# Query products of a linear-attention block on a block diagonal with a doubled k^T v, in a fused attention and two-stage MoE kernel

## The chip, the cores and the metric

The kernel runs on one core of a Trainium2 chip. The metric is the device time of one execution in microseconds. A NeuronCore has five engines that run on their own: TensorE (PE, with its weight loads listed as PEld), VectorE (DVE), ScalarE (ACT), GpSimd (POOL) and SyncE (SP, here the queue that issues most transfers).

## The reference, cut to what matters

Eight batches of eight heads go through linear attention without softmax, then through an RMS norm per head. The result feeds a first mixture of experts (top 1 of 8, routed by a cosine) and a second one (a balanced assignment).

```python
def _attn_ref(q, k, v, g_norm):          # q, k, v: (8, 8, 576, 64) float32
    kv = np.einsum('bhsd,bhse->bhde', k, v)
    out = np.einsum('bhsd,bhde->bhse', q, kv)
    rms = np.sqrt(np.mean(out * out, axis=-1, keepdims=True) + 1e-06)
    return (out / rms * g_norm).astype(np.float32)
...
    x = np.ascontiguousarray(attn_out.transpose(0, 2, 1, 3)).reshape(B * S, H * D)
    x = _moe_ref(x=x, **moe_kwargs)      # logits = normed x @ normed expert_emb.T / tau
    return _moe2_ref(x=x, **moe2_kwargs)
```

## The kernel before

The kernel is one function with nested helpers; all instructions are issued in program order, and each engine works through its own in that order. The attention part is at the start of the span, up to about 141 us; the two mixtures of experts fill the rest.

**k^T v.** Batches are handled in four groups of two (gi = 0 to 3). For each batch, `kv(b)` (L255) multiplies the 576 rows of k and v of each head in nine chunks of 64 rows (L265, matmuls on 64x64 quarters of the array), four heads to a PSUM tile, two such halves per batch (hg). ACT copies a half to the tile `kvn` (L272), and for the first half DVE copies it a second time (L274). Then eight matmuls per batch (L287, 64 rows by 128 columns of weights, 80 columns moving) multiply it by `gex`. `gex` (L210, filled by `gate_weights` at L230 to L237) holds, beside an identity, the routing vectors of the experts for two heads. So one product both moves k^T v into place and multiplies it by the routing weights. DVE and ACT copy its halves to `kvx` (L291, L292), one of four buffers that batches use in turn. `kvh` (L251) picks the columns of one head in one half of the partitions: 64 columns of k^T v and 8 columns of logits, KW = 72 in all.

**Query products.** A step is one unit: one pair of 128-row blocks (u = 0 to 3, four heads hg) or a tail of 64 rows per batch (u = 4). There are ten steps per group, forty in all, listed by `steps`. `qa` (L299) transposes four 128x128 blocks of q on PE (L310); each transposed block has two rows of a token pair r = 0, 1 above one another, so partitions 0 to 63 belong to r = 0 and 64 to 127 to r = 1. ACT copies them to `qT` (L311). `qb` (L314) multiplies for each head h and each r a 64x128 block of weights from `qT` with the 72 columns of `kvh` (L329, eight matmuls per unit; for u = 4 L336 with 64x64 blocks). Every f32 matmul that is not a transpose shows in the trace as two loads and two matmul passes, so a unit has sixteen of each. The PSUM pool `mm` that holds products, k^T v and later the expert layers has two buffers.

**Evacuation.** DVE or ACT (a list `EVAC` decides) copies the values to `x` (L347, L349), ACT squares them (L352) and copies the logits to `lp` (L355), and one step later DVE sums the squares (L359, `late`). In the last group ACT does the copy of every unit.

**Order.** Step n first starts a `kv` of the next group at the steps named in `KVAT`, transposes for step n + 2 (`qa`), issues loads of q, then runs `qb` of step n, then one piece of every generator in `bg` (`pump`): `kv` and `group_end`. `group_end` (L363) makes the norm, the routing and the slot tables of the group before on DVE, POOL and PE (L467, L468, L507). In the last group the steps also cast the first expert weights (ACT L553, DVE L559). After the steps, `first0` (L949) fills PE with the first expert's layers (L678 to L680, L720 to L722) while DVE and POOL finish the tables and the gathers, and the transposes L645 take the gathered rows. `warm` (L849, L852) runs transposes at the start. At the start POOL also fills constants (L188, L581, L699) and token numbers (L860, L863) that DVE splits (`split64`, L866).

The groups of 64-row matmuls differ in array shape: transposes and expert layers use 128x128, L329 and L287 use 64x128, L265 and L336 use 64x64.

Of the kernel before, what the change touches and what calls it, by code (L numbers as in the profile page):

```python
# [7 lines left out]
F32 = mybir.dt.float32  # L8
# [3 lines left out]
AF = mybir.ActivationFunctionType  # L12
OP = mybir.AluOpType
AX = mybir.AxisListType
# [57 lines left out]
def fused_kernel(ctx, tc, q, k, v, g_norm, emb, tau, w1, w2, wgate, v1, v2, out):  # L72
    nc = tc.nc
    V = nc.vector
    B, H, S, D = q.shape
    HD = H * D
    HP = H // 2
    E = emb.shape[0]
# [22 lines left out]
    def mk(pool, shape, dtype, name, **kw):  # L101
        if pool is mp:
            pool = MP[name in MP0]
        return pool.tile(shape, dtype, name=name, **kw)

    def con(shape, dtype, name):
        return consts.tile(shape, dtype, name=name)
# [8 lines left out]
    gp = grp.enter_context(tc.tile_pool(name="grp", bufs=1, side="right"))  # L116
    att = ExitStack()
    ap = att.enter_context(tc.tile_pool(name="att", bufs=2, side="right"))
# [49 lines left out]
    ident = con([128, 128], F32, "ident")  # L168
# [26 lines left out]
    def run_gen(g):  # L195
        for _ in g:
            pass

    def rsqrt(o, u, y, w):

        nc.scalar.activation(w, u, AF.Sqrt)
        yield
        V.reciprocal(y, w)
        V.tensor_tensor(w, u, y, op=OP.mult)
        V.scalar_tensor_tensor(w, w, -0.5, y, op0=OP.mult, op1=OP.mult)
        V.scalar_tensor_tensor(o, w, 1.5, y, op0=OP.add, op1=OP.mult)

    gex = mk(gp, [128, 2, E + D + E], F32, "gex")  # L210

    def gate_weights():
        emsq = mk(ap, [128, 8, D], F32, "sq").rearrange("p a c -> p (a c)")[:E, :HD]
        en2 = con([E, 4], F32, "en2")
        V.tensor_tensor(emsq, em, em, op=OP.mult)
        V.tensor_reduce(en2[:, 0:1], emsq, axis=AX.X, op=OP.add)
        V.tensor_scalar(en2[:, 1:2], en2[:, 0:1], 1e-36, None, op0=OP.max)
        run_gen(rsqrt(en2[:, 2:3], en2[:, 1:2], en2[:, 3:4], emsq[:, 0:1]))
        V.tensor_tensor(en2[:, 0:1], en2[:, 0:1], en2[:, 2:3], op=OP.mult)
        V.tensor_scalar(en2[:, 0:1], en2[:, 0:1], 1e-6, tau8, op0=OP.add, op1=OP.mult)  # L220
        V.reciprocal(en2[:, 0:1], en2[:, 0:1])
        emh = em.rearrange("p (h d) -> p h d", h=H)
        V.scalar_tensor_tensor(emh, emh, en2[:, 0:1], gB[:E, None, :].to_broadcast([E, H, D]),
                               op0=OP.mult, op1=OP.mult)
        yield
        pe_ = mk(psum, [64, H, E], F32, "sm")
        for h in range(H):
            nc.tensor.transpose(pe_[:, h, :], em[:, h * D:(h + 1) * D], ident[:E, :E])

        for c in range(2):  # L230
            V.tensor_copy(gex[64 * c:64 * c + 64, :, E:E + D],
                          ident[64 * c:64 * c + 64, None, 64 * c:64 * c + 64].to_broadcast([64, 2, D]))
            for s in range(2):
                h = 2 * (c ^ s) + s
                g = gex[64 * c:64 * c + 64, s]
                V.tensor_copy(g[:, :E], pe_[:, h])
                V.tensor_copy(g[:, E + D:], pe_[:, h + 4])  # L237


    KW = D + E  # L240
# [4 lines left out]
    V.memset(run, 0.0)  # L245
    NKV = 4


    kvx = [mk(ap, [128, 2, 2, 2, KW + E], F32, f"kvx{i}", bufs=1) for i in range(NKV)]

    def kvh(b, h, r):  # L251
        hg, a, s = h // 4, h // 2 % 2, h % 2
        return kvx[b % NKV][64 * r:64 * r + 64, a ^ s, s, hg ^ r, E * hg:E * hg + KW]

    def kv(b):  # L255

        kvn = mk(ap, [128, 2, 3, D], F32, "kvn", bufs=2)
        for hg in range(2):
            p = mk(psum, [128, 2, 512], F32, "mm")
            kt, vt = LD["k", b, hg], LD["v", b, hg]  # L260
            for r in range(KR):
                for s in range(2):
                    for a in range(2):
                        c = s ^ a
                        nc.tensor.matmul(p[64 * c:64 * c + 64, s, :D],  # L265
                                         vt[64 * s:64 * s + 64, a, r, :], kt[64 * s:64 * s + 64, a, r, :],
                                         start=(r == 0), stop=(r == KR - 1))
            m = 2 * b + hg + NL
            if m < 2 * B:
                load_main(m // 2, "k", m % 2)  # L270
                load_main(m // 2, "v", m % 2)
            nc.scalar.copy(kvn[:, :, hg], p[:, :, :D])  # L272
            if hg == 0:
                V.tensor_copy(kvn[:, :, 2], p[:, :, :D])  # L274
            yield
            if hg == 0:
                yield
        if b > 0:
            yield

        W = KW + E
        p = mk(psum, [128, 2, 512], F32, "mm")
        for s in range(2):
            for o in range(2):
                for c in range(2):
                    i = 2 * s + o
                    nc.tensor.matmul(p[:, c, i * W:(i + 1) * W],  # L287
                                     kvn[64 * c:64 * c + 64, s, o:o + 2].rearrange("p h d -> p (h d)"),
                                     gex[64 * c:64 * c + 64, s], start=True, stop=True)
        x = kvx[b % NKV].rearrange("p c s o w -> p c (s o w)")  # L290
        V.tensor_copy(x[:, 0], p[:, 0, :4 * W])  # L291
        nc.scalar.copy(x[:, 1], p[:, 1, :4 * W])  # L292
        yield

    GS = {}
# [18 lines left out]
    def qb(gi, u, hg, late):  # L314
        if u == 0 and hg == 0:
            GS[gi] = dict(s1=mk(gp, [128, TG * H], F32, "s1", bufs=2), lp=mk(gp, [128, TG * H, E], F32, "lp", bufs=2))
        if hg == 0:
            GS[gi]["x", u] = mk(gp, [128, 2, XP], F32, "xo", bufs=8) if u < 4 else mk(gp, [128, 1, XP], F32, "xt", bufs=2)
        G = GS[gi]
        j, rr = divmod(u, 2)  # L320
        qT = QT.pop((gi, u, hg))
        po = mk(psum, [128, 2, 512], F32, "mm")
        n = 8 if u < 4 else 4
        if u < 4:

            ov = po[:, :, :4 * KW].rearrange("p r (h w) -> p r h w", h=4)
            for h in range(4):
                for r in range(2):
                    nc.tensor.matmul(ov[:, r, h], qT[64 * r:64 * r + 64, h, :], kvh(2 * gi + j, 4 * hg + h, r),  # L329
                                     start=True, stop=True)  # L330
        else:
            ov = po[:, :, :2 * KW].rearrange("p a (c w) -> p a c w", w=KW)
            for h in range(2):
                for s in range(2):
                    for jj in range(2):
                        nc.tensor.matmul(ov[64 * jj:64 * jj + 64, s, h],  # L336
                                         qT[64 * s:64 * s + 64, h, 64 * jj:64 * jj + 64],
                                         kvh(2 * gi + jj, 4 * hg + 2 * h + s, s), start=True, stop=True)

        vs, ls = (slice(E, KW), slice(0, E)) if hg == 0 else (slice(0, D), slice(D, KW))  # L340
        o3 = po[:, :, :n // 2 * KW].rearrange("p a (c w) -> p a c w", w=KW)
        sq = mk(ap, [128, 8, D], F32, "sq")
        x = G["x", u]
        c0 = u * 16 + hg * n
        cp = nc.scalar.copy if (gi, u, hg) in EVAC else V.tensor_copy
        if u < 4:
            cp(x[:, :, hg * 4 * D:(hg + 1) * 4 * D].rearrange("p r (h d) -> p r h d", h=4), ov[:, :, :, vs])  # L347
        else:
            cp(x[:, 0, hg * 4 * D:(hg + 1) * 4 * D].rearrange("p (c s d) -> p s c d", s=2, c=2), ov[:, :, :, vs])  # L349
        if late is not None:  # L350
            late()
        nc.scalar.activation(sq[:, :n].rearrange("p (a c) d -> p a c d", a=2), o3[:, :, :, vs], AF.Square)  # L352

        o = "p (c a) n -> p a c n" if u < 4 else "p (a c) n -> p a c n"
        nc.scalar.copy(G["lp"][:, c0:c0 + n].rearrange(o, a=2), o3[:, :, :, ls])  # L355

        def later():
            o = "p (c a) -> p a c" if u < 4 else "p (a c) -> p a c"
            V.tensor_reduce(G["s1"][:, c0:c0 + n].rearrange(o, a=2), sq[:, :n].rearrange("p (a c) d -> p a c d", a=2),  # L359
                            axis=AX.X, op=OP.add)  # L360
        return later

    def group_end(gi):  # L363
# [534 lines left out]
    for n, st in enumerate(steps):  # L898
        gi, u, hg = st
        i = n % len(UNITS)  # L900
# [502 lines left out]
    a = logits_w(e6, 0)  # L1403
    xtiles(0, e7, 2, 3)
    a()
    b = logits_w(e6, 1)
# [99 lines left out]
    a = logits_w(e7, 1)  # L1506
# [182 lines left out]
```

## Time and profile before

| what | value |
|---|---|
| runs shown | median 1156.23 us, 1155.98 to 1157.61, three runs |
| profiled execution | 1156.87 us, its span 1155.1 us |
| PE busy | 1106.5 us (96%), 8819 matmuls |
| DVE, ACT, POOL busy | 618.5, 448.7, 299.0 us |
| mean granted TensorE clock | 0.95 of full |
| bytes moved | 153.03 MB, mean 132 GB/s |

A busy time is the union of an engine's instructions. Matmuls overlap, so a PE that is busy all the time need not be at its peak; the granted clock (1.0 is 2.4 GHz, 0.5 is 1.2 GHz) is shown beside it. In a line of the timeline the first number is the start in us from the span's start, the second how long the merged run lasts, and square brackets give idle time of the engine before it and what ended it. "issue" means that the engine waited for nothing that the profile shows.

### The profile page before, as it was taken

To read this page: it belongs to the slowest core of one execution; us is meant where nothing else is said; L and a number is where in the kernel's file an instruction comes from. 1 tells how busy PE (TensorE), PEld (TensorE's weight loads), DVE (VectorE), ACT (ScalarE), POOL (GpSimd) and SP (SyncE) were. 2 spreads that over 40 slices of the span, in tenths; PEclk is the share of its full clock that TensorE was granted. 3 is DMA by queue.
4 is the path that set the end of the run, shared out by engine and by line. 5 is a ranking of instruction groups with operands and counts; after the bars stand their busy time and mean duration, and the time that the engine had idled before them with its cause. 6 is when DMAs were issued, how large, how long until landed. Compare 5 with 4: busy or idle time off the path is not lost. (4 is left out here: it accounts for less than half of the span.)

```text
span 1155.1 us, 21545 instructions
## 1 busy us (share of the span) xinstructions
PE 1106.5 (96%) x8819; PEld 1019.8 (88%) x8819; DVE 618.5 (54%) x1319; ACT 448.7 (39%) x801; POOL 299.0 (26%) x374
## 2 busy tenths in 40 slices
PE   8899997999999999999989988999999999999998
PEld 7677787999999999999879878989898998989896
DVE  3366875387778686868546671615243433425140
ACT  2365635543535363545431221424233332425130
POOL 0011436425142332415003332112213030203101
PEclk8787588999999999999999888999999999999999
DMA  9997545442525343434120123515153433424201
GB/s 286 380 341 243 197 143 176 137 144 83 175 88 160 103 145 118 128 115 129 55 77 2 44 75 99 159 60 188 55 174 99 147 119 112 140 90 156 87 29 41
DMA packets 94532, 153.03 MB, mean 132 GB/s; under 512 B 11080, under 2 KB 52040, under 8 KB 94416
## 3 DMA queue, kind: packets, MB, share of 16 engines
q1 hardware_dynamic: 85456, 122.18, 33.1%
q0 software_dynamic: 8960, 29.30, 7.9%
q8 instruction: 73, 1.20, 0.4%
q14 instruction: 43, 0.35, 0.1%
HBM read 121.63 MB, written 29.82 MB: 131 GB/s over the span
## 5 line engine op out<-in xcount | busy, mean ns | idle before, releaser
L678 PE MATMUL mm<-xh,whi 128*128 128x256 f32 (+2 forms) x1024 | 311.1, 304 | 2.9 <-DVE hl L696 1.5
L679 PE MATMUL mm<-xl,whi 128*128 128x256 f32 (+2 forms) x1024 | 307.9, 301 | 1.1 <-DVE ti L655 0.9
L680 PE MATMUL mm<-xh,wlo 128*128 128x256 f32 (+2 forms) x1024 | 307.5, 300 | 0.0
L678 PEld LDWEIGHTS mm<-xh,whi 128*128 128x128 f32 x1024 | 194.9, 190 | 5.5 <-ACT xh L648 2.0
L679 PEld LDWEIGHTS mm<-xl,whi 128*128 128x128 f32 x1024 | 194.9, 190 | 1.9 <-DVE ti L655 1.3
L680 PEld LDWEIGHTS mm<-xh,wlo 128*128 128x128 f32 x1024 | 194.8, 190 | 0.0
L559 DVE TENSOR_TENSOR wlo<-wraw,whi 128x1024 fp32r<-128x1024 f32 x124 | 153.7, 1239 | 50.8 <-ACT whi L553 49.1
L720 PE MATMUL mm<-hh,whi 128*128 128x352 f32 (+1 forms) x512 | 161.4, 315 | 3.3 <-PEq L1509 3.3
L649 DVE TENSOR_TENSOR xl<-tp,xh 128x512 fp32r<-128x512 f32 (+2 forms) x80 | 51.5, 649 | 197.1 <-ACT xh L648 197.1
L722 PE MATMUL mm<-hh,wlo 128*128 128x352 f32 (+1 forms) x512 | 157.0, 307 | 0.0
L721 PE MATMUL mm<-hl,whi 128*128 128x352 f32 (+1 forms) x512 | 156.8, 306 | 0.0
L553 ACT CAST whi<-wraw 128x1024 fp32r<-128x1024 f32 x128 | 133.3, 1043 | 0.0
L1630 POOL DMA_INDIRECT out<-yr,ti x40 | 39.3, 982 | 315.9 <-ACT yr L1628 293.1
L810 DVE SCALAR_TENSOR_TENSOR rc<-xg,big 128x512 bf16<-128x512 f32 x128 | 111.7, 873 | 2.6
L720 PEld LDWEIGHTS mm<-hh,whi 128*128 128x128 f32 x512 | 98.9, 193 | 5.3 <-issue 4.1
L1617 PE MATMUL mm<-whi,hh 128*128 128x512 f32 x256 | 101.6, 397 | 0.0
L1619 PE MATMUL mm<-whi,hl 128*128 128x512 f32 x256 | 101.0, 394 | 0.0
L1618 PE MATMUL mm<-wlo,hh 128*128 128x512 f32 x256 | 100.9, 394 | 0.0
L695 ACT ACTIVATE hh<-mm 128x512 fp32r<-128x512 f32 (+1 forms) x88 | 57.1, 649 | 111.5 <-PE mm L680 111.5
L721 PEld LDWEIGHTS mm<-hl,whi 128*128 128x128 f32 x512 | 99.4, 194 | 0.0
L722 PEld LDWEIGHTS mm<-hh,wlo 128*128 128x128 f32 x512 | 99.2, 194 | 0.0
L726 ACT COPY yT<-mm 128x512 f32<-128x512 f32 (+1 forms) x32 | 21.3, 667 | 193.6 <-PE mm L722 193.6
(275 smaller groups left out, 1598.8 us busy)
## 6 DMA issues: line engine op xcount, KB each, us to landing
wraw<-in_moe_w SPq DMA_DIRECT2D x128, 512.0 KB, 3.7
kmain<-in_k SPq DMA_DIRECT2D x16, 576.0 KB, 9.0
vmain<-in_v SPq DMA_DIRECT2D x16, 576.0 KB, 9.9
xbuf<-xo SPq DMA_DIRECT2D x16, 528.0 KB, 7.7
ybuf<-yr SPq DMA_DIRECT2D x32, 260.0 KB, 2.1
qmain<-in_q SPq DMA_DIRECT2D x16, 512.0 KB, 10.1
xg<-in_moe_w SPq DMA_DIRECT2D x16, 256.0 KB, 3.3
xg<-in_moe_w_gate SPq DMA_DIRECT2D x8, 256.0 KB, 4.1
```

The costliest lines, as they stand in the source:

```text
L553: nc.scalar.copy(hi, raw)
L559: eng.tensor_tensor(lo, raw, hi.bitcast(F32), op=OP.subtract)
L678: nc.tensor.matmul(o, a, xh[:, kd, :N], start=(kd == 0), stop=False)
L679: nc.tensor.matmul(o, a, xl[:, kd, :N], start=False, stop=False)
L680: nc.tensor.matmul(o, b, xh[:, kd, :N], start=False, stop=(kd == KD - 1))
L720: nc.tensor.matmul(o, a, hh[:, kf, :N], start=(kf == 0), stop=False)
L721: nc.tensor.matmul(o, a, hl[:, kf, :N], start=False, stop=False)
L722: nc.tensor.matmul(o, b, hh[:, kf, :N], start=False, stop=(kf == KF - 1))
L810: V.scalar_tensor_tensor(junk, raws[i], 1.0, wgB[:, x], op0=OP.mult, op1=OP.mult, accum_out=w2g[:, i // KF, i % KF, x:x + 1])
L1617: nc.tensor.matmul(ps[:n, i, :], hh, a, start=(kf == 0), stop=False)
L1618: nc.tensor.matmul(ps[:n, i, :], hh, b, start=False, stop=False)
L1619: nc.tensor.matmul(ps[:n, i, :], hl, a, start=False, stop=(kf == KF - 1))
```

## The change

The query product of a head becomes one matmul over all 128 partitions instead of two over 64. For that `kvx` holds each head's 64 + 8 columns twice, on a block diagonal: partitions 0 to 63 with columns r = 0, partitions 64 to 127 with columns r = 1, zeros elsewhere. The zeros are written once by POOL for the four buffers; the copies after L287 write only the diagonal blocks. To get k^T v on both halves of the partitions, `kvn` holds each head's block twice side by side (one ACT copy with a broadcast for each half, and no DVE copy). `gex` gets one identity for each of its four blocks instead of one between two routing blocks, so a product of L287 has 72 columns instead of 80. The output of a unit now has the order (bank a, head c, r) instead of (r, head), so the access patterns of the evacuation change and its element counts don't. The tail units use the diagonal blocks with 64x64 matmuls as before.

```diff
-    gex = mk(gp, [128, 2, E + D + E], F32, "gex")
+    gex = mk(gp, [128, 2, 2, D + E], F32, "gex")
...
         for c in range(2):
-            V.tensor_copy(gex[64 * c:64 * c + 64, :, E:E + D],
-                          ident[64 * c:64 * c + 64, None, 64 * c:64 * c + 64].to_broadcast([64, 2, D]))
             for s in range(2):
                 h = 2 * (c ^ s) + s
                 g = gex[64 * c:64 * c + 64, s]
-                V.tensor_copy(g[:, :E], pe_[:, h])
-                V.tensor_copy(g[:, E + D:], pe_[:, h + 4])
+                V.tensor_copy(g[:, :, :D], ident[64 * c:64 * c + 64, None, 64 * c:64 * c + 64].to_broadcast([64, 2, D]))
+                V.tensor_copy(g[:, :, D:], pe_[:, h:h + 5:4])
...
-    kvx = [mk(ap, [128, 2, 2, 2, KW + E], F32, f"kvx{i}", bufs=1) for i in range(NKV)]
-
-    def kvh(b, h, r):
+    kvx = [mk(ap, [128, 2, 4, 2, KW], F32, f"kvx{i}", bufs=1) for i in range(NKV)]
+    for t in kvx:
+        nc.gpsimd.memset(t, 0.0)
+
+    def kvh(b, h):
         hg, a, s = h // 4, h // 2 % 2, h % 2
-        return kvx[b % NKV][64 * r:64 * r + 64, a ^ s, s, hg ^ r, E * hg:E * hg + KW]
+        return kvx[b % NKV][:, a ^ s, 2 * s + hg]
...
-        kvn = mk(ap, [128, 2, 3, D], F32, "kvn", bufs=2)
+        kvn = mk(ap, [128, 2, 2, 2, D], F32, "kvn", bufs=2)
...
-            nc.scalar.copy(kvn[:, :, hg], p[:, :, :D])
-            if hg == 0:
-                V.tensor_copy(kvn[:, :, 2], p[:, :, :D])
+            nc.scalar.copy(kvn[:, :, hg], p[:, :, None, :D].to_broadcast([128, 2, 2, D]))
...
-        W = KW + E
         p = mk(psum, [128, 2, 512], F32, "mm")
-        for s in range(2):
-            for o in range(2):
-                for c in range(2):
-                    i = 2 * s + o
-                    nc.tensor.matmul(p[:, c, i * W:(i + 1) * W],
-                                     kvn[64 * c:64 * c + 64, s, o:o + 2].rearrange("p h d -> p (h d)"),
-                                     gex[64 * c:64 * c + 64, s], start=True, stop=True)
-        x = kvx[b % NKV].rearrange("p c s o w -> p c (s o w)")
-        V.tensor_copy(x[:, 0], p[:, 0, :4 * W])
-        nc.scalar.copy(x[:, 1], p[:, 1, :4 * W])
+        for i in range(4):
+            for c in range(2):
+                nc.tensor.matmul(p[:, c, i * KW:(i + 1) * KW],
+                                 kvn[64 * c:64 * c + 64, i // 2, i % 2].rearrange("p u d -> p (u d)"),
+                                 gex[64 * c:64 * c + 64, i // 2, i % 2], start=True, stop=True)
+        x = kvx[b % NKV]
+        for r in range(2):
+            (nc.scalar.copy if r else V.tensor_copy)(x[64 * r:64 * r + 64, :, :, r],
+                p[64 * r:64 * r + 64, :, :4 * KW].rearrange("p c (i w) -> p c i w", w=KW))
...
         if u < 4:
-
-            ov = po[:, :, :4 * KW].rearrange("p r (h w) -> p r h w", h=4)
+            ov = po[:, :, :4 * KW].rearrange("p a (h r w) -> p a h r w", h=2, r=2)
             for h in range(4):
-                for r in range(2):
-                    nc.tensor.matmul(ov[:, r, h], qT[64 * r:64 * r + 64, h, :], kvh(2 * gi + j, 4 * hg + h, r),
-                                     start=True, stop=True)
+                nc.tensor.matmul(ov[:, h // 2, h % 2], qT[:, h, :], kvh(2 * gi + j, 4 * hg + h), start=True, stop=True)
         else:
...
-                                         kvh(2 * gi + jj, 4 * hg + 2 * h + s, s), start=True, stop=True)
-
-        vs, ls = (slice(E, KW), slice(0, E)) if hg == 0 else (slice(0, D), slice(D, KW))
+                                         kvh(2 * gi + jj, 4 * hg + 2 * h + s)[64 * s:64 * s + 64, s], start=True, stop=True)
...
-            cp(x[:, :, hg * 4 * D:(hg + 1) * 4 * D].rearrange("p r (h d) -> p r h d", h=4), ov[:, :, :, vs])
+            cp(x[:, :, hg * 4 * D:(hg + 1) * 4 * D].rearrange("p r (a c d) -> p a c r d", a=2, c=2), ov[:, :, :, :, 0:D])
...
```

The rest of the diff replaces the column slices `vs` and `ls` of the tail copy, the squares, the logits and the sums by 0:D and D:KW, and drops the reordering views of `lp` and `s1`.

## Rows read from the trace of the kernel before

**Rows 1.** The page: busy time of engines (section 1), granted clock by slice (section 2).
```profile
PE 1106.5 (96%) x8819; PEld 1019.8 (88%) x8819; DVE 618.5 (54%) x1319; ACT 448.7 (39%) x801; POOL 299.0 (26%) x374
...
PEclk8787588999999999999999888999999999999999
```

**Rows 2.** Busy time by stretch: length; PE, PEld, DVE, ACT, POOL; clock; DMA.
```profile
46.00:56.20 10.20, 10.20 (x145) 8.68 (x149) 4.11 (x8) 3.47 (x11) 0.00 (x0) 0.51 1.07 379
56.30:80.00 23.70, 21.60 (x510) 18.45 (x504) 17.05 (x44) 15.02 (x41) 3.02 (x12) 1.00 1.07 348
80.20:90.30 10.10, 10.10 (x148) 8.64 (x142) 2.03 (x6) 4.27 (x13) 0.00 (x0) 0.51 0.98 304
...
107.50:151.70 44.20, 41.59 (x318) 35.15 (x318) 33.98 (x85) 24.91 (x63) 15.56 (x32) 0.50 0.60 194
...
107.50:116.40 8.90, 8.90 (x79) 7.04 (x78) 5.20 (x8) 5.43 (x14) 1.54 (x2) 0.50 0.85 233
```

**Rows 3.** Timeline of PE, 40 to 108 us: the three long idle times.
```profile
45.83 1.13 PE L329 MATMUL mm<-kvx,qT 64*128 64x72 f32 x7 [1.90 <-issue]
...
79.21 0.60 PE L310 MATMUL tp<-ident,qmain 128*128 128x128 f32 x4 [1.34 <-DMA xbuf<-xo]
...
107.09 0.43 PE L265 MATMUL mm<-kmain,vmain 64*64 64x64 f32 x3 [1.87 <-issue]
```

**Rows 4.** Timeline of PE around 150 us: expert products on either side of a clock change.
```profile
146.91 0.41 PE L678 MATMUL mm<-xh,whi 128*128 128x256 f32 x1
...
151.93 0.28 PE L680 MATMUL mm<-xh,wlo 128*128 128x256 f32 x1
```

**Rows 5.** Timeline of PE near 61 us: one unit at full clock.
```profile
60.93 1.11 PE L329 MATMUL mm<-kvx,qT 64*128 64x72 f32 x16
61.98 0.66 PE L310 MATMUL tp<-ident,qmain 128*128 128x128 f32 x4
62.56 1.11 PE L329 MATMUL mm<-kvx,qT 64*128 64x72 f32 x16
```

**Rows 6.** Timeline of PE near 120 us: one unit at half clock.
```profile
119.95 1.99 PE L329 MATMUL mm<-kvx,qT 64*128 64x72 f32 x16
121.87 1.12 PE L310 MATMUL tp<-ident,qmain 128*128 128x128 f32 x4
122.92 1.99 PE L329 MATMUL mm<-kvx,qT 64*128 64x72 f32 x16
```

**Rows 7.** Timeline of the weight loads, 24 to 28 us: 72 and 80 moving columns.
```profile
24.25 0.97 PEld L329 LDWEIGHTS mm<-kvx,qT 64*128 64x128 f32 x16 [0.17 <-ACT kvn L272]
...
27.98 0.98 PEld L287 LDWEIGHTS mm<-gex,kvn 64*128 64x128 f32 x16
```

**Rows 8.** Timeline of PE near 557 us: f32 products of 256 columns, four side by side.
```profile
557.05 0.63 PE L822 MATMUL sm<-hl,w2g 128*32 128x256 f32 x8
557.48 0.65 PE L822 MATMUL sm<-hh,w2g 128*32 128x256 f32 x8
```

**Rows 9.** Timeline of PE near 209 us: transposes between products of the same array shape.
```profile
209.08 0.33 PE L722 MATMUL mm<-hh,wlo 128*128 128x352 f32 x1
209.24 0.60 PE L645 MATMUL tp<-ident,xg 128*128 128x128 f32 x4
209.60 0.41 PE L720 MATMUL mm<-hh,whi 128*128 128x352 f32 x1
209.84 0.33 PE L721 MATMUL mm<-hl,whi 128*128 128x352 f32 x1
```

**Rows 10.** Groups by line and shape: copies of k^T v, first 240 us; a memset, first 20.
```profile
L272 ACT COPY kvn<-mm 128x128 f32<-128x128 f32 x16 | 4.4, 275 | 19.8 <-PE mm L265 19.7
...
L291 DVE COPY kvx<-mm 128x320 f32<-128x320 f32 x8 | 3.9, 488 | 7.5 <-PE mm L287 7.5
...
L274 DVE COPY kvn<-mm 128x128 f32<-128x128 f32 x8 | 2.3, 292 | 12.4 <-ACT kvn L272 12.4
...
L699 POOL MEMSET L<- 128x320 f32 x1 | 0.4, 392 | 0.0
```

More of the change, by code (lines that the diff above doesn't have):

```diff
@@ L346, in qb @@
         if u < 4:
-            cp(x[:, :, hg * 4 * D:(hg + 1) * 4 * D].rearrange("p r (h d) -> p r h d", h=4), ov[:, :, :, vs])
+            cp(x[:, :, hg * 4 * D:(hg + 1) * 4 * D].rearrange("p r (a c d) -> p a c r d", a=2, c=2), ov[:, :, :, :, 0:D])
         else:
-            cp(x[:, 0, hg * 4 * D:(hg + 1) * 4 * D].rearrange("p (c s d) -> p s c d", s=2, c=2), ov[:, :, :, vs])
+            cp(x[:, 0, hg * 4 * D:(hg + 1) * 4 * D].rearrange("p (c s d) -> p s c d", s=2, c=2), ov[:, :, :, 0:D])
         if late is not None:
             late()
-        nc.scalar.activation(sq[:, :n].rearrange("p (a c) d -> p a c d", a=2), o3[:, :, :, vs], AF.Square)
-        o = "p (c a) n -> p a c n" if u < 4 else "p (a c) n -> p a c n"
-        nc.scalar.copy(G["lp"][:, c0:c0 + n].rearrange(o, a=2), o3[:, :, :, ls])
+        nc.scalar.activation(sq[:, :n].rearrange("p (a c) d -> p a c d", a=2), o3[:, :, :, 0:D], AF.Square)
+        nc.scalar.copy(G["lp"][:, c0:c0 + n].rearrange("p (a c) n -> p a c n", a=2), o3[:, :, :, D:KW])
         def later():
-            o = "p (c a) -> p a c" if u < 4 else "p (a c) -> p a c"
-            V.tensor_reduce(G["s1"][:, c0:c0 + n].rearrange(o, a=2), sq[:, :n].rearrange("p (a c) d -> p a c d", a=2),
-                            axis=AX.X, op=OP.add)
+            V.tensor_reduce(G["s1"][:, c0:c0 + n], sq[:, :n], axis=AX.X, op=OP.add)
         return later
```

## The prediction

> **What bounds the kernel now.** I read the page first. PE is busy 96% of the span, so a change to PE work can count; but the clock line shows 5s, 7s and 8s in the first seven slices of 29 us and almost only 9s later [rows 1]. The attention part, which the change touches, is where PE runs slow. I then cut the stretches so that each has one clock level [rows 2]. PE is busy all of 46.0 to 56.2 and 80.2 to 90.3 us at 0.5, and 41.6 of the 44.2 us from 107.5 to 151.7 at 0.5 (1.2 GHz); between them it runs at 1.0 (2.4 GHz). No other engine is full in the slow stretches: DVE 4.1 of 10.2, 2.0 of 10.1 and 34.0 of 44.2 us. So in the first two PE at half clock is the bound, and in the third it is PE first, with DVE close behind.
>
> Why is the clock low there? Ahead of each slow stretch PE stands idle for 1.3 to 1.9 us [rows 3], put down to "issue", once to a store. These are the only PE gaps of over a microsecond between 40 and 140 us. After them PE works without a pause and the clock still does not come back for 10, 10 and 44 us. It comes back at 151.8 us, after a run of expert products of 256 columns that follow one another every 0.21 us at half clock, from 146.91 us on, and drop to 0.12 us [rows 4]. So work that looks busy in the trace did not bring the clock back, and denser work did. The next question is how dense the query products are.
>
> At full clock a unit takes 62.56 - 60.93 = 1.63 us, of which 1.05 us lie from the first query product to the first transpose and 0.58 us are for four transposes [rows 5]. At half clock it takes 122.92 - 119.95 = 2.97 us: 1.92 and 1.05 [rows 6]. The weight loads of a unit last 0.97 us for 72 moving columns, and those of L287 0.98 us for 80 [rows 7]. So the moving columns don't set the pace. The sixteen loads go in eight pairs, one for each half of the partitions; with 0.19 us for the last, a pair comes every (0.97 - 0.19)/7 = 0.112 us, and the columns stream inside that time. How long they stream shows where weights are small: eight f32 passes of 256 columns, four side by side, take 0.43 us [rows 8], so 0.215 us for 256, 0.84 ns a column. 72 columns stream for 60 ns of 112: before the change, the array waits for weights nearly half of each pass.
>
> **The change, part by part.** *Query products.* 32 units (u below 4) have sixteen passes less sixteen, that is eight passes of 144 columns: 144 x 0.84 = 121 ns at full clock against 112, since loading 128 columns of weights (107 to 112 ns) now hides behind the stream. Eight passes: 0.97 us against 0.89, +0.07. At half clock 1.94 against 1.71 (loads at twice 107 ns), +0.23. From below: if the wider product streamed at half that price a column, the load would set the pace and the change is 0; from above: see the rival. I take 121 ns, since the transposes below fit the same price.
>
> *Gaps between array shapes.* A transpose of 128 columns streams for 128 x 0.84 = 108 ns. 0.58 us for four of them leaves 0.15 us, and 1.05 us for eight pairs of 0.112 us leaves another 0.15 us. Where transposes stand between products of their own shape, the five matmuls from 209.24 to 209.84 take 0.60 us, which is four times 0.108 and one matmul of 0.16 (209.08 to 209.24), and nothing is left [rows 9]. So the gap belongs to the switch from 128x128 to 64x128, not to the wait for qT. After the change a unit has no switch: 0.44 + 0.97 + 0.04 for the rest = 1.45 us against 1.63, -0.18. At half clock 0.86 + 1.94 = 2.80 against 2.97, -0.17. Beside a product L265 (64x64) one gap stays, and I count -0.05. Between 33 and 107 us there are about ten units of each kind: -2.3 us; I take -2, since DVE is busy 17 of 23.7 us in 56 to 80 [rows 2].
>
> *The clock.* A unit after the change streams for 0.43 + 0.97 of its 1.45 us, like the expert products that brought the clock back. I expect the stalls of rows 3 to remain in some form (PE issues 256 loads and 256 matmuls less, which moves them; the sign is unknown), the clock to fall after them, but to return after a few us. Ceiling for 46.0 to 56.2 and 80.2 to 90.3: 20.3/2 = 10.2 us; floor 0. I take -4, since the first part after each stall stays slow. For 107.5 to 116.4 (PE 8.9 of 8.9, DVE 5.2 [rows 2]) the ceiling is 4.5; I take -2.5 for the same reason. For 116.4 to 151.7 DVE was busy 33.98 - 5.20 = 28.8 of 35.3 us, so at most 6.5 us can go before DVE's own queue (tables of group 2 and 3, sums, weight splits L559) is the bound; I take -4. What is late next there is DVE's L359, which PE cannot outrun by more than the two PSUM buffers and the two `sq` buffers.
>
> *Copies.* DVE loses eight copies of 0.29 us (L274), and ACT's sixteen copies of 0.275 us double in size [rows 10]: between 0 and +0.275 each; 320 columns of L291 against 128 of L274 cost 0.20 us more for 192, 1 ns a column, so I take +0.13, 2.1 us in all. The next product in the other `mm` buffer waits for that copy; for the first halves the serial DVE copy behind it is gone, for the second halves 0.13 us is added: 0 in sum. `kvx`: 576 elements on 64 partitions instead of 320 on 128, between 0.49 and 0.49 x 576/320 = 0.88 us; I take 0.75 by the same 1 ns a column. A batch's `kvx` is read several units later, so this is hidden in seven of eight batches. For batch 0 it delays the first unit by up to 0.5 us; the loads of k and v that PE meets next bound that start, so I take 0, and +0.5 without that cover.
>
> *Zeros.* Four memsets of 1152 columns on POOL: between 0.39 us each (as for 320, [rows 10]) and 0.39 x 3.6 = 1.4. At most 5.6 us at the start, ahead of the token numbers that DVE splits (L866). What DVE does next is to fill `gex`, and that waits for PE's transposes L228 behind the first k^T v, whose loads have to land; after that POOL has nothing for a long while (0.00 from 46.0 to 56.2 us [rows 2]). So 0 is taken; without that cover up to 5.6 us. `gex` trades ten small copies for eight: 0. No transfer is added or moved past another; loads of k, v and q are tied to PE as before.
>
> **Sum.** -2 - 4 - 2.5 - 4 = -12.5 us. The profiled execution took 1156.87 us, 1.8 more than its span and 0.6 above the median; 1156.9 - 12.5 = 1144.4.
>
> **The rivals.** *The clock stays low.* The products are denser, but the stretch from 107.5 us stays at 0.5, since what brought the clock back were other products. Then only the gaps go: -2 and 12 slow units of 0.17, -4 in all: 1152.9. For it: one instance of a rise was read. Against: transposes and products would be one unbroken stream. Chance 0.10.
>
> *DVE takes over early.* The clock rises, but DVE's queue behind group ends (34 of 44.2 us) gives back most of it and only the first two slow stretches pay: about -6, 1151. For it: DVE is busy 17 of 23.7 us even where the clock is full. Against: it idles at 80 to 90 us. Chance 0.12.
>
> *The columns set the pass after all.* Two halves of 72 columns run side by side now; one full product gives that up. If a pass lasted 112 ns because of its 72 columns, 144 would need 223 ns: 8 x 0.11 = +0.9 us a unit, 32 units: +28, 1185 us. The place is L329 alone, and it decides if its eight passes take over 1.3 us at full clock. Against: 80 columns took the time of 72 [rows 7]. Chance 0.04. A page's rule says the same: the Trainium skill, "TensorEngine Tiling (Array Packing)", section Theoretical Speedup, gives row tiling up to twice the speed for a contraction of 64 or less, which this change undoes; rows 7 agree that the pairs run together, but show the gain eaten by the weight loads. By that rule alone the sum would be +28 instead of -12.5.
>
> *The stalls land worse.* Same units, but one or two more stalls of 1.9 us, each with a slow stretch behind it of 3 to 5 us lost, eat the gain: 1156 to 1161. Chance 0.06.
>
> **How the numbers follow.** Forecast 0.68 at 1144.4. The low end takes all ceilings: -3 - 10.2 - 4.5 - 6.5 = -24, partly hidden, 1134; the high end is the clock rival with one more stall, 1156. Two tenths stay outside. What a measurement of this kernel can tell from no change is about 0.2%, 2.3 us. Faster by more: the forecast, the DVE rival and about half of the clock rival, less a little for losses not seen, 0.82; within: 0.08; slower: 0.10.
>
> **What would show it.** In the profile after, L329 must show eight loads and eight passes per unit with a unit near 1.45 us at full clock; no gap of 0.15 us beside its transposes; a clock of mostly 1.0 between 107 us and the end of attention, and the expert products of rows 4 some 10 us earlier than 146.91. Units of over 1.63 us at full clock, or a clock of 0.5 through the last group with PE busy, would make the forecast wrong; so would expert products that start as early as forecast, with later DVE waits that take it back.

## The result and the profile after

The changed kernel took 1145.03 us (median of 4 runs, 1143.17 to 1150.37) against 1156.3 us for the kernel before (4 runs beside it). The ratio is 0.9911, with a 95% interval of 0.9883 to 0.9939: 11.3 us less, where 12.5 were forecast. The profiled execution is the slowest of the four, 1150.37 us with a span of 1148.6, so its trace shows less than the median gain; a step read from it is named as such.

The page after, busy time by engine and granted clock by slice, stands against [rows 1]:

```profile
PE 1091.8 (95%) x8563; PEld 1011.2 (88%) x8563; DVE 618.9 (54%) x1309; ACT 451.6 (39%) x801; POOL 303.4 (26%) x378
...
PEclk8998798999999999999989888999999999999999
```

PE lost 256 products and 256 loads, and 14.7 us of busy time. The first seven digits of the clock were 8787588 and are now 8998798. The busy time by stretch (length; PE, PEld, DVE, ACT, POOL; clock; DMA), cut again where the clock changes, stands against [rows 2]:

```profile
33.00:63.00 30.00, 26.41 (x615) 23.08 (x614) 17.43 (x35) 17.87 (x46) 1.47 (x10) 1.00 1.07 355
63.60:67.00 3.40, 3.40 (x18) 3.39 (x17) 1.28 (x2) 1.24 (x4) 0.00 (x0) 0.54 1.07 344
67.00:104.40 37.40, 32.09 (x682) 28.11 (x681) 26.60 (x64) 25.76 (x66) 2.97 (x12) 1.00 1.05 353
104.60:111.20 6.60, 6.60 (x53) 5.90 (x54) 3.32 (x6) 4.39 (x11) 1.54 (x2) 0.51 0.69 151
111.40:124.90 13.50, 9.14 (x76) 8.48 (x72) 12.46 (x29) 9.58 (x22) 9.20 (x16) 0.99 0.63 199
125.10:142.00 16.90, 12.49 (x83) 10.71 (x83) 15.24 (x47) 8.41 (x24) 4.52 (x14) 0.51 0.58 204
```

The two slow stretches of ten microseconds are gone: between 33 and 104 us there is one of 3.4 us. The third, 44 us long before, has become 6.6 us, a stretch at full clock, and 16.9 us. In the stretch at full clock PE is busy 9.1 of 13.5 us and DVE 12.5: the bound there has changed engine.

The timeline of PE after shows the units [rows 5, 6], what the stalls of [rows 3] became, and the first expert transposes (start, length, what ran; in brackets the idle time ahead and what ended it):

```profile
29.16 1.43 PE L264 MATMUL mm<-kmain,vmain 64*64 64x64 f32 x41 [2.69 <-issue]
...
62.14 0.79 PE L264 MATMUL mm<-kmain,vmain 64*64 64x64 f32 x34 [2.03 <-issue]
...
63.40 2.13 PE L322 MATMUL mm<-kvx,qT 128*128 128x144 f32 x8
65.32 1.06 PE L305 MATMUL tp<-ident,qmain 128*128 128x128 f32 x4
...
104.51 1.99 PE L281 MATMUL mm<-gex,kvn 64*128 64x72 f32 x16 [2.19 <-ACT lp L344]
...
111.83 1.15 PE L322 MATMUL mm<-kvx,qT 128*128 128x144 f32 x8
112.81 0.60 PE L305 MATMUL tp<-ident,qmain 128*128 128x128 f32 x4
113.25 1.15 PE L322 MATMUL mm<-kvx,qT 128*128 128x144 f32 x8
...
126.33 0.69 PE L305 MATMUL tp<-ident,qtail 128*128 128x128 f32 x2 [3.52 <-ACT qT L306]
...
131.79 1.97 PE L632 MATMUL tp<-ident,xg 128*128 128x128 f32 x8
```

A unit at full clock is 113.25 - 111.83 = 1.42 us: 0.98 from the first product to the first transpose, 0.44 for four transposes, and no gap beside either. At half clock the products take 65.32 - 63.40 = 1.92 us. Two stalls put down to "issue", of 2.69 and 2.03 us, are still there, and behind each the clock is at 0.5; but it is back after some 3.4 us (29.2 to 32.6 and 63.6 to 67.0 us), where [rows 2] had ten twice. The kernel before had one of that length too, from 32.1 to 35.5 us at 0.50; only products of k and v and transposes ran in it. The stretch at 0.50 near the start, mostly the first k^T v, is as long as before (12.6 to 22.4 us, 12.0 to 21.5 before). The first expert transposes start at 131.79 us instead of 141.00.

The copies, by line and shape over the first 240 us (busy time, mean ns of one; idle time before), against [rows 10]:

```profile
L271 ACT COPY kvn<-mm 128x256 f32<-128x256 f32 x16 | 6.1, 384 | 18.6 <-PE mm L264 18.5
...
L286 DVE COPY kvx<-mm 64x576 f32<-64x576 f32 x8 | 6.0, 746 | 4.9 <-PE mm L281 4.9
L286 ACT COPY kvx<-mm 64x576 f32<-64x576 f32 x8 | 5.1, 634 | 9.3 <-DVE kvx L286 9.3
...
L248 POOL MEMSET kvx<- 128x1152 f32 x4 | 4.2, 1097 | 0.0
```

### The profile page after: what moved, and what is told of

It reads as the page before. It is cut to its first block, busy times and chain, and to the rows that moved or that the text cites. A ratio compares the mean times of both kernels' runs of the same rounds, so it can differ in the third digit from the quotient of the medians.

```text
span 1148.6 us, 21025 instructions
## 1 busy us (share of the span) xinstructions
PE 1091.8 (95%) x8563; PEld 1011.2 (88%) x8563; DVE 618.9 (54%) x1309; ACT 451.6 (39%) x801; POOL 303.4 (26%) x378
```

## The experiments

The theory: the gain comes from the query products alone. As full-array products of 144 columns they make a unit without array switches, and with them the clock comes back sooner after a stall. Against it stood that the gain comes from the edits around them (eight DVE copies fewer, other layouts), that the missing array switch alone does it, and, for the end of attention, that DVE's queue is the bound whatever PE does.

**Products back to pairs, all else kept.** The layouts of `kvn` and `kvx`, the copies and the zeros stay as after the change; the zero halves are written and not read.

```
-                nc.tensor.matmul(ov[:, h // 2, h % 2], qT[:, h, :], kvh(2 * gi + j, 4 * hg + h), start=True, stop=True)
+                for r in range(2):
+                    nc.tensor.matmul(ov[:, r, h], qT[64 * r:64 * r + 64, h, :],
+                                     kvh(2 * gi + j, 4 * hg + h)[64 * r:64 * r + 64, r], start=True, stop=True)
```

> The kernel after the change with the query products alone put back: two 64x128 matmuls of 72 columns a head, each reading its diagonal block. The doubled buffers, the zeros, the broadcast copy and the 72-column routing product stay. Theory (the products' shape and density give the gain): back to before, 1154 to 1159 us, a unit of 1.63 us at full clock with sixteen loads, long stretches at 0.5 with PE busy. Rival (the gain comes from the DVE copies that went, or from the other edits): stays at 1143 to 1148 us.

It took 1157.99 us against 1156.38: ratio 1.003 (1.000 to 1.006). The whole gain is gone. Its profiled execution, at 1152.59 us, is the fastest of its ten (the slowest took 1167.37). Its stretches and one unit:

```profile
34.60:54.80 20.20, 19.27 (x310) 16.97 (x309) 4.60 (x7) 6.84 (x18) 0.00 (x0) 0.50 1.06 380
...
106.20:147.00 40.80, 37.25 (x291) 31.58 (x291) 32.58 (x82) 23.88 (x59) 15.54 (x32) 0.50 0.56 181
```

```profile
116.45 1.99 PE L323 MATMUL mm<-kvx,qT 64*128 64x72 f32 x16
118.37 1.12 PE L305 MATMUL tp<-ident,qmain 128*128 128x128 f32 x4
119.42 1.99 PE L323 MATMUL mm<-kvx,qT 64*128 64x72 f32 x16
```

The unit is 2.97 us again [rows 6], and the long stretches at 0.5 with PE busy are back, 20 and 41 us. The copies, the zeros and the other layouts bring no gain by themselves.

**Each product cut in two, over all 128 rows.** Same array shape and no switch, but 72 columns to a pass, and twice as many passes.

```
+                for r in range(2):
+                    nc.tensor.matmul(ov[:, h // 2, h % 2, r], qT[:, h, :], kvh(2 * gi + j, 4 * hg + h)[:, r],
+                                     start=True, stop=True)
```

> The kernel after the change with each 144-column product cut into two of 72 columns over the same 128 partitions, so sixteen loads and sixteen passes a unit as before, one array shape as after. Both theories: a unit at full clock of 16 x 0.112 + 0.44 + 0.04 = 2.27 us with no gap of 0.15 us beside the transposes. Theory (density of the stream brings the clock back): passes stream 60 of 112 ns as before, so the clock stays at 0.5 after stalls with PE busy, 1176 to 1195 us. Rival (what brings it back is that all 128 rows are in use): clock as after the change, mostly 1.0, and about 0.85 us a unit more than after, part of it hidden in the last group, 1160 to 1172 us.

1160.61 us, ratio 1.0029 (1.0006 to 1.0052). The theory's 1176 to 1195 us failed; the time, and the clock of mostly 1.0 from 33 us on, are what its rival had (all 128 rows in use). In its trace:

```profile
65.42 1.90 PE L323 MATMUL mm<-kvx,qT 128*128 128x72 f32 x16
67.16 0.60 PE L305 MATMUL tp<-ident,qmain 128*128 128x128 f32 x4
67.60 1.90 PE L323 MATMUL mm<-kvx,qT 128*128 128x72 f32 x16
```

```profile
13.00:33.00 20.00, 19.37 (x287) 18.27 (x280) 3.73 (x11) 5.02 (x11) 0.00 (x0) 0.50 1.09 338
33.20:118.40 85.20, 80.09 (x1540) 74.06 (x1539) 47.12 (x103) 47.81 (x120) 6.02 (x24) 1.00 0.94 304
```

A unit costs 2.18 us at full clock (2.27 forecast), 0.55 more than the old pairs (1.63): sixteen passes of 0.109 us, each about as long as a pair of loads in [rows 7] (0.112). Yet the total is only 0.3% above before. 32 units at 0.55 us are 17.6 us of PE work more at full clock, and the median lies some 4 us above before: some 13 us, by that estimate, don't show in the total. The clock, higher than before from 50 us on, and PE's waits in the last group, which longer units fill, can both account for them; no run separates the two. So two effects stand beside each other, the pitch of a unit and the clock.

After 20 us at 0.5 the clock stays at 1.00 for 85 us, with PE busy 80 of them. That is a clock held rather than got back: PE has no pause of over 1.0 us from 33 us up to 114 us, and behind the first, 1.43 us ahead of 116.18, the clock is at 0.51 from 118.6 to 125.2 us. What set it free at 33 and at 125 us in this kernel is open. The two studies of single shapes below do not explain it, and the first speaks against the rival.

**Four shapes by themselves.** To see which stream brings the clock back, four stretches were added ahead of attention, each behind a pause of 9 to 10 us; nothing is left out, and the added products go nowhere. Its time is not compared.

```
+    for shape, n in (("pair", 40), ("unit", 24), ("full72", 40), ("full144", 36)):
+        stretch(shape, n)
```

> The kernel before with four stretches of matmuls put in front of the attention, each after a pause of PE of several us, on constant data, their results not used: 40 pairs of 64x128 matmuls of 72 columns without anything between; six units as before (four transposes, four pairs); 40 matmuls of 72 columns over all 128 partitions; 36 of 144 columns over all 128 partitions. Each would last some 17 us at 0.5. The time is not compared. Theory 1 (the share of time in which columns stream brings the clock back): the first three all stream about 0.6 of the time and stay at 0.5 to their end, only the 144-column stretch rises to 1.0 within some 7 us. Theory 2 (matmuls over all 128 rows bring it back, halves don't): the third and the fourth stretch rise, the pairs and the units stay at 0.5. Theory 3 (the switches of array shape keep it low): all rise but the units.

Stretches of its trace: pairs of 72 columns, units of transposes and pairs, 72 columns over 128 rows, then 144 columns over 128 rows in two lines.

```profile
19.00:36.40 17.40, 17.28 (x161) 17.15 (x161) 0.06 (x1) 0.00 (x0) 0.00 (x0) 0.50 0.59 167
46.80:63.50 16.70, 16.70 (x116) 14.26 (x116) 0.00 (x0) 0.00 (x0) 0.00 (x0) 0.50 0.01 1
73.80:91.00 17.20, 17.20 (x80) 17.13 (x80) 0.00 (x0) 0.00 (x0) 0.00 (x0) 0.50 0.00 1
101.40:104.80 3.40, 3.36 (x14) 3.39 (x15) 0.00 (x0) 0.00 (x0) 0.00 (x0) 0.52 0.00 0
105.00:112.00 7.00, 7.00 (x58) 6.87 (x57) 0.00 (x0) 0.00 (x0) 0.00 (x0) 1.00 0.01 2
```

Three shapes keep PE busy without a pause for 17 us, and the clock stays at 0.50. The 144-column products get it back after 3.4 us. All four went as Theory 1 said. 72 columns over all 128 rows, the third line, stay at 0.50, so using all rows is not enough here. A rise like the one that the prediction had read once in [rows 4] is seen here by itself.

**Columns or rows?** Three more stretches: pairs of 144 columns on both halves, 144 columns on the upper 64 rows alone, and units of four transposes with eight 72-column products over 128 rows.

```
+    for shape, n in (("pair144", 36), ("half144", 36), ("unit72", 48)):
+        stretch(shape, n)
```

> Three more stretches of matmuls in front of the attention of the kernel before, each after a pause of PE, results not used, the time not compared: 36 pairs of 64x128 matmuls of 144 columns, both halves; 36 matmuls of 144 columns on the upper 64 rows alone; six units of the kind of the two-times-72 kernel (four transposes, eight matmuls of 72 columns over 128 rows, one array shape). If the share of time in which columns stream decides: the first two rise to 1.0 within some 7 us, the third stays at 0.5 or rises late. If the part of the array in use counts as well: the first rises, the second, with half the rows, stays at 0.5. If only matmuls over all 128 rows bring the clock back: the first two stay at 0.5.

In that order, two lines for the first shape:

```profile
19.00:24.00 5.00, 4.94 (x52) 4.95 (x54) 0.00 (x0) 0.00 (x0) 0.00 (x0) 0.64 1.14 336
24.00:29.00 5.00, 5.00 (x86) 5.00 (x86) 0.00 (x0) 0.00 (x0) 0.00 (x0) 1.00 0.87 236
40.00:50.00 10.00, 9.80 (x41) 9.83 (x42) 0.05 (x1) 0.00 (x0) 0.00 (x0) 0.50 0.01 2
70.00:80.00 10.00, 10.00 (x50) 10.00 (x50) 0.00 (x0) 0.00 (x0) 0.00 (x0) 0.50 0.00 0
```

Pairs of 144 columns on both halves bring the clock back in under 5 us; the same columns on one half leave it at 0.50, and so do units with 72 columns on all rows. That is the second of the three outcomes; the first, Theory 1 of the experiment above, and the third fail. So, among the stretches tried, neither the pairing nor the 144 columns nor the 128 rows by itself tells those that rise from those that don't; of the edits of this kernel, the change from pairs of 72 to products of 144 goes from one kind to the other. The page "TensorE: Matmul & The Clock Gate" of the Trainium skill, Part 1, says that activity releases the throttle; these rows show that unbroken PE work of some shapes does not.

**A burst ahead of the old pairs.** Before the change, plus 32 transposes of the identity ahead of the unit at 112 us, which go nowhere.

```
+        if n == 29:
+            warm(32)
```

> The kernel before with 32 more transposes of the identity ahead of the query product of step 29, some 6.8 us of unbroken 128x128 work at 0.5, results not used. Theory (the pairs hold the clock where it is high but don't bring it back): the clock rises to 1.0 within the burst or just behind it, near 120 us, and holds for at least 10 us while units of the old kind take 1.63 us or wait for DVE; the attention ends as late as before or up to 3 us later, 1154 to 1160 us in all. Rival (units of the old kind pull the clock down by themselves): back at 0.5 within 4 to 7 us after the burst, units of 2.97 us again, 1160 to 1165 us.

1157.05 us in one run, beside 1154.7 to 1162.75 of before. Its stretches, from the second half of the burst on:

```profile
114.00:116.40 2.40, 2.40 (x24) 2.28 (x21) 0.68 (x2) 0.00 (x0) 0.00 (x0) 1.00 0.34 31
116.50:127.70 11.20, 10.25 (x140) 8.80 (x139) 8.40 (x21) 9.33 (x23) 5.99 (x14) 0.99 0.40 137
127.80:148.00 20.20, 14.42 (x114) 12.13 (x113) 18.61 (x50) 10.05 (x27) 7.06 (x13) 0.50 0.55 200
```

Units of the old kind keep the clock for 11 us once the burst has raised it, and are then 1.63 us long also in this stretch; by themselves they didn't raise it in the 17 us of the experiment on four shapes. (In the kernel before it did come back twice, after ten microseconds in which 64x64 products and the products L287 ran beside them [rows 2].) From 127.8 us on DVE is busy 18.6 of 20.2 us and PE 14.4. The first expert transposes start at 139.18 us (141.00 before), and the one total lies among those of before.

**The changed kernel again, and its end.** Two more runs of the changed kernel, and two edits of the end of attention: other steps for the weight splits and one load, and nine transposes of the identity ahead of each of four late units, so that the clock doesn't fall.

> The kernel after the change once more, as the measure for the next one: 1143 to 1147 us in the median. If the spread comes from where the clock falls between 557 and 700 us, its profiled execution has another set of stretches at 0.5 there than the first.

> The kernel after the change a third time, on the chip of the run before it, as its measure: 1142 to 1148 us in the median.

```
-CASTS = {25: 0, 26: 0, 28: 0, 32: 0, 34: 0, 36: 0}
-LOADS = {19: 1, 21: 2, 23: 3, 27: 4, 30: 5, 31: 6, 33: 7, 35: 8}
+CASTS = {25: 0, 26: 0, 28: 0, 29: 0, 35: 0, 37: 0}
+LOADS = {19: 1, 21: 2, 23: 3, 27: 4, 30: 5, 31: 6, 33: 7, 36: 8}
```

> The kernel after the change with three weight casts of the last steps moved: the one of step 32 to step 29, those of 34 and 36 to 35 and 37 (one load goes a step later with them). Theory (in the last group DVE's queue is now the bound, and ACT's square root waits behind a weight split): two splits of 1.2 us leave DVE's queue ahead of the first norm of the last group, the PE wait of 3.5 us near 123 us falls under 1.5 us, the clock stays up, and the time is 2 to 6 us under the kernel after. Rival (another wait takes its place, since DVE's work has only moved): within 1.5 us of the kernel after.

```
+        if n in (35, 36, 37, 38):
+            warm(9)
```

> The kernel after the change with nine transposes of the identity ahead of the transposes of each of the steps 35 to 38, where PE waited for ACT and DVE, results not used. Theory (DVE's queue bounds the last steps, so PE has time to spare there): the clock stays at 1.0 from about 112 us on or falls for under 7 us instead of 17, and the time is 0 to 3 us under the kernel after (1142 to 1145 us), since the tables on DVE set the end of this part. Rival (PE's extra 1 us a step adds to the path): 2 to 4 us over the kernel after.

The changed kernel took 1144.88 us (1139.26 to 1150.04), ratio 0.9913 (0.9887 to 0.9938), and 1146.05 (1142.42 to 1150.19), 0.9904 (0.9878 to 0.9929). The other split steps: 1146.64, 0.992 (0.9893 to 0.9946). The 2 to 6 us hoped for are not there, and the trace shows the rival: the wait of 3.52 us becomes one of 1.58 us ahead of 124.38, but one of 2.61 us for ACT's logits stands ahead of 131.14, and the first expert transposes start at 131.83 us, where they were (131.79). The fill: 1145.05, 0.9876 (0.9836 to 0.9916); the kernel before took 1158.54 beside it, the interval overlaps those of the changed kernel, and in microseconds the two are equal, so no gain is shown. The fill did what it was for:

```profile
125.10:135.00 9.90, 5.07 (x68) 4.12 (x68) 8.76 (x23) 7.38 (x22) 3.32 (x6) 1.00 0.76 268
135.20:142.00 6.80, 6.46 (x29) 6.07 (x30) 5.64 (x24) 0.81 (x4) 1.20 (x8) 0.52 0.36 147
```

Of the 16.9 us at half clock in the profile after (the last stretch shown there) 6.8 are left, and yet the last gathers start at 153.19 us, where the changed kernel had 153.90 and, the third time, 153.32. PE is busy 5.1 of 9.9 us at full clock and DVE 8.8. So PE's clock doesn't set the end of attention; that DVE's queue does, as forecast, fits these numbers, but no run took work off it without adding work elsewhere.

**DVE's work to POOL.** If DVE is the bound, a split and a late split less on it should pay: one split and the first late one go to POOL, the second late one is left to the next, `PEW[5]`, which sets the place of the last table product (L494) in PE's stream, is lowered, and the fill stays (seven transposes).

```
-LATEC = (0, 0, 0, 0)
-PEW = (0.0, 0.85, 1.55, 0.75, 2.5, 4.5, 2.2)
-CASTS = {25: 0, 26: 0, 28: 0, 32: 0, 34: 0, 36: 0}
+LATEC = (1, 0, 0, 0)
+PEW = (0.0, 0.85, 1.55, 0.75, 2.5, 2.5, 2.2)
+CASTS = {25: 0, 26: 0, 28: 0, 29: 0, 34: 1, 36: 0}
...
-            late_cast(nc.gpsimd if LATEC[f] else V)
+            if f != 1:
+                late_cast(nc.gpsimd if LATEC[f] else V)
```

> The kernel after the change with work taken off DVE's queue in the last steps and behind them: the weight cast of step 32 goes to step 29, the weight splits of step 34 and of the first expert tile go from DVE to POOL, the last split comes one tile later, the place of the last table product in PE's stream moves up by 2 us, and seven transposes of the identity stand ahead of the steps 35 to 38. Theory (DVE's queue from 112 to 150 us sets when the last gather starts): the chain to the last gather loses two to three splits of 1.2 us, the first of the three last gathers starts 2 to 4 us earlier than 153.9 us (counted with this run's own earlier stalls), and the time is 1.5 to 4 us under the kernel after. Rival (POOL's splits hold DVE up, or PE's place in the stream decides): within 1 us of the kernel after.

1158.71 us, ratio 1.002 (1.0002 to 1.0038): the gain is lost. The timelines of DVE, POOL and PE:

```profile
123.06 2.33 DVE L463 TENSOR_TENSOR run<-run,bs 128x8 f32<-128x8 f32 x1
...
156.95 0.69 DVE L683 SCALAR_TENSOR_TENSOR hl<-mm,hh 128x512 fp32r<-128x512 f32 x1 [3.81 <-ACT hh L682]
```

```profile
123.00 2.37 POOL L546 TENSOR_TENSOR wlo<-wraw,whi 128x1024 fp32r<-128x1024 f32 x1
...
149.53 2.52 POOL L488 TENSOR_TENSOR oha<-oh,tokhl 128x360 bf16<-128x360 bf16 x2 [2.92 <-DVE oh L485]
...
158.02 1.01 POOL L614 DMA_INDIRECT xg<-xbuf,tabi  x1 [5.96 <-DVE tabi L881]
```

```profile
152.11 0.76 PE L494 MATMUL sm<-oha,ohb 128*128 128x80 bf16 x9 [3.25 <-POOL oha L488]
```

A sum over 8 columns, 0.17 us in the profile after, takes 2.33 us on DVE and ends with the split that POOL began 0.06 us earlier. What DVE saves on the split (1.22 us) it loses on the sum. The page "SBUF — State Buffer" of the Trainium skill, section Who interferes with whom, says that a DVE instruction with two SBUF inputs contends with a GpSimd instruction that reads SBUF, over a port pair that is locked exclusively. The two ends, 125.39 and 125.37 us, agree.

By itself this loses nothing: POOL's table product L488 starts at 149.53 us, and at 149.51 in the changed kernel beside it (the third run). What is lost comes behind it. L488 takes 2.52 us instead of 1.54. PE, which now comes to its product L494 earlier, waits 3.25 us for it where it waited 0.61, and the clock is at 0.57 from 152 to 156 us. The expert products, ACT's `hh` and DVE's L683 come late by that, and behind L683 in DVE's queue stands the index of the gathers (L881): DVE idles 3.81 us, and the last gathers start at 158.02 us instead of 153.90 (153.32 in the run beside it). The rest of some 13 us is not followed here; the clock is at 0.51 once more from 166 to 172.6 us. So both halves of the rival were there, POOL's splits and PE's place in the stream, and the edit changed them together, so that their shares are not told apart. None of the edits tried on top of the changed kernel beat it beyond the noise.

## Why the prediction was right

The forecast was 1144.4 us; the runs gave 1145.03, 1144.88 and 1146.05. By steps:

- **The pass of 144 columns** was to cost 121 ns, and a unit 1.45 us. Measured: 0.98/8 = 122 ns and 1.42 us. At half clock the products were to take 1.94 us and took 1.92. The gap of 0.15 us beside transposes is gone. The columns' rival (1185 us) falls: 1.42 us is below the 1.63 of the pairs, not 0.9 above. The rule of the page "TensorEngine Tiling (Array Packing)" of the Trainium skill, section Theoretical Speedup, up to twice the speed, would have given that rival's time; here a pair took 112 ns and the one product in its place 122.
- **Gaps, 33 to 107 us, -2 us, and the two slow stretches, -4 us.** A unit at full clock is 0.21 us shorter instead of 0.18. In the profiled run the lead over before goes from 0 at 40.5 us to 6.3 at 102.9: it grows by 4.6 us across 46 to 56 us and by 4.6 across 80 to 90, and 2.9 us are lost again to the stall at 60.1 us and the slow stretch behind it (from 4.34 to 1.47). So the two terms met their sum, 6.3 us for 6, but not their shares. Where both kernels run at full clock the lead doesn't grow by 0.2 us a unit (1.47 to 1.99 us from 67.6 to 76.8, 6.54 to 6.26 from 90.5 to 102.9): the gaps show in the unit and hardly in the sum, and the slow stretches, sized at 4, gave nearly all.
- **107.5 to 116.4, -2.5 us.** About -1, too large by 1.5: PE waited 2.19 us for ACT's logits ahead of 104.51 us, and the clock was 0.51 to 111.2 us. The ceiling was halved for a first slow part after a stall, and the slow part took more than that.
- **116.4 to 151.7, -4 us, then DVE.** The lead grew by 5.6 us and gave back 3.3. Net -2.3, less than forecast by 1.7. The lead fell at PE's wait of 3.52 us. The working named L359 as what is late next. The queue was right, the instruction was not, as the timelines of DVE and ACT show:

```profile
124.23 1.22 DVE L546 TENSOR_TENSOR wlo<-wraw,whi 128x1024 fp32r<-128x1024 f32 x1
125.37 0.17 DVE L385 TENSOR_SCALAR uu<-s 128x32 f32<-128x32 f32 x1
```

```profile
125.58 0.23 ACT L201 ACTIVATE ww<-uu 128x32 f32<-128x32 f32 x1 [3.12 <-DVE uu L385]
125.71 0.57 ACT L306 COPY qT<-tp 128x512 f32<-128x512 f32 x1
```

  PE's wait of 3.52 us ahead of 126.33 is for ACT's copy of qT; ACT stood 3.12 us at a small activation for DVE's L385, which stood behind a weight split of 1.22 us.
- **Copies, 0.** The kvn copy takes 0.384 us (0.405 forecast), kvx 0.746 and 0.634 (0.75), a memset 1.10 (0.39 to 1.4). The run with the pairs, which keeps all of these, is within 0.3% of before: 0, or slightly worse, is right.
- **Expert transposes and products some 10 us earlier.** They are 9.1 to 9.4 us earlier in the profiled run, and so are the last gathers (153.90 for 163.26), so later DVE waits do not take it back. The first expert transposes, in one profiled execution each, with the mean clock of three stretches:

| kernel | 12 to 50 us | 50 to 100 us | 100 to 160 us | transposes start | its own time |
|---|---|---|---|---|---|
| before | 0.77 | 0.84 | 0.63 | 141.00 | 1156.87 |
| pairs, all else after | 0.79 | 0.95 | 0.66 | 137.49 | 1152.59 |
| 72 columns, 128 rows | 0.73 | 1.00 | 0.86 | 143.57 | 1161.43 |
| after | 0.82 | 0.97 | 0.80 | 131.79 | 1150.37 |
| after, again | 1.00 | 0.99 | 0.83 | 124.75 | 1139.26 |
| after, a third time | 0.82 | 0.97 | 0.80 | 130.88 | 1150.19 |

The rivals. *The clock stays low*: in the profile after it comes back within 3.4 and 6.6 us, except at the end. There the prediction's own sign, a clock of mostly 1.0 from 107 us to the end of attention, is only half met: 13.5 of some 25 us. *DVE takes over early*: fits the last 20 us, where the fill and the moved splits changed nothing; but beside the first two stretches, which paid its -6, the later ones paid 3.3 more. *The stalls land worse*: ahead of the first expert transposes PE pauses eight times for over a microsecond, from 9 us on, where before had seven, and the longest are longer; but they cost less, since the clock returns.

The mechanism held, and that the number is met within 1 us is in part luck. In the profiled run one term is too small by 2.3 and three are too large by some 5 together, so attention gave 9.6 us instead of 12.5. And the profiled run, the slowest of its four, doesn't keep all of its lead. It is 9.9 us ahead of before from 200 to 569 us, and 6.5 after 721 us, which fits 1156.87 - 1150.37. The median, at which the forecast aimed, has no profile of its own. The clock in that later part was 0.90 after and 0.94 before; first after, then before:

```profile
557.00:640.00 83.00, 77.43 (x595) 71.03 (x594) 49.05 (x142) 19.65 (x31) 19.49 (x15) 0.90 0.11 37
```

```profile
557.00:640.00 83.00, 78.21 (x651) 69.89 (x641) 44.86 (x142) 22.36 (x38) 15.43 (x12) 0.94 0.10 34
```

The program there is the same, so where the clock falls differs from run to run. The second profile of the changed kernel has other stretches at 0.5 there, as its expectation said (a mean of 0.92 instead of 0.88 from 680 to 722 us), but that is the smaller part of the spread: of the 11.1 us between 1150.37 and 1139.26, 7.0 are there at the first expert transposes (131.79 and 124.75), behind a clock of 0.82 and 1.00 from 12 to 50 us. Nor is each pause followed by a fall: in the kernel before PE stood idle 1.68 us ahead of 39.37 us, and the clock was 1.00 up to 44 us. What decides where the stalls ("issue") land, and behind which of them the clock falls, was not tried.

## What to carry to other kernels

Where the granted clock is 0.5 and PE looks busy, put that work behind a pause by itself and see whether the clock comes back, then try the wider form: a product that multiplies by zeros won here, mostly where the clock now comes back, though each pass got a little longer. Price an edit of small products by the pitch of a unit (first product to next first product), with weight loads and array switches in it, rather than by columns. A gain on one engine lasts up to the next engine's queue, so name the instruction that will be late there, not the queue alone, and before giving DVE's work to POOL look at which small DVE instructions will run beside it. Change one place in a queue at a time: the last experiment changed two and can't tell their costs apart.

## What the runs showed of the hardware that was not expected

Unbroken PE work for 17 us left the clock at 0.50 in four of the shapes tried (pairs of 72 columns, units of transposes and pairs, 72 columns on 128 rows, 144 columns on 64 rows) and units of transposes with 72-column products on 128 rows did so for over 20 us; 144 columns on both halves got it back in under 5 us, in pairs or in one. A DVE instruction of 0.17 us took 2.33 us beside a POOL split. And leaving out 256 products and loads did not take away PE's stalls put down to "issue": 2.69 and 2.03 us stand in the profile after, 1.90 and 1.87 in [rows 3].
